# A new step table for one core that runs a gated linear-attention block and a gated MLP: another order and other engines for the same steps

## The chip, the core and the metric

The kernel runs on one core of one Trainium2 chip. Five engines work side by side, each through its own row of instructions, strictly in that row's order: TensorE (PE: matrix products and transposes, with its weight loads PEld), VectorE (DVE), ScalarE (ACT), GpSimd (POOL) and SyncE (SP, which here issues nearly all DMA transfers; ACT issues a few). An instruction waits until the steps that it depends on are done, and everything behind it in its engine's row waits with it. The metric is the device time of one execution in microseconds (us), as the median of several runs.

## What is computed

One transformer block with adaptive modulation, for 2048 rows of width 448 (bf16), cut to its core:

```python
mod = (silu(c) @ w_mod).reshape(1, 6, 1, 448)        # sa, ca, ga, sb, cb, gb
h = layernorm(x) * (1 + ca) + sa
q, k, v = split(h @ wqkv)                            # 16 heads of 28
phi = lambda t: concat(softmax(t @ w_phi), softmax(-(t @ w_phi)))
kv, z = einsum(phi(k), v), sum(phi(k))
o = phi(q) @ kv / (phi(q) @ z + 1e-6)
x = x + ga * (o @ wo)
h = layernorm(x) * (1 + cb) + sb
z1, z2 = split(gelu(h @ w_in))                       # 2 x 896
g = w_sp @ layernorm(z2) + b_sp                      # mixes the 2048 rows
x = x + gb * ((z1 * g) @ w_out)
```

## The kernel before

Everything stays on the chip between the stages. The 2048 rows are 16 tiles of 128 rows, and two tiles form a pair, so most loops run over 8 pairs. The function `fast_path` has one small function for each step, and the string `ORDER` (a step table) lists all steps of the program in one sequence. The loop at its end walks through `ORDER` and issues each step's instructions; every engine's row is thus the table read for that engine alone. A word is `step:arguments@bank/engine`: `kP:7,1/V` is step kP of pair 7, tile 1, on VectorE (V DVE, S ACT, G POOL, Y SP), `kM:0@A1` uses the two PSUM banks A1. A bank is free again only when the step that reads it out is done. DMA completion is told by a ring of eight semaphores: a transfer that is issued later in the table waits until the one eight places before it has landed.

The steps that matter below, in the order of the stages:

- **Start.** `ld:x0` to `x5` bring x (tiles 0, 1, 2-3, 4-7, 8-11, 12-15), `wq`, `wk`, `phi`, `v0` to `v3` the attention weights, `wca`, `wsa`, `wcb`, `wsb` four sixths of w_mod (wcb lands in the place of wca, wsb in that of wsa). `du` and `dh` are products of zeros that only keep TensorE busy. `ct` turns c, `ce` makes silu(c), `cf` (32 products) computes one sixth of the modulation, `ec` copies it out. `FTk`/`FTq` transpose wk and wq (line 817), `ETk`/`ETq` copy them out (821 on ACT, 823 on DVE), `bd` spreads phi over a block diagonal, `PFk`/`PFq` multiply (835), `EPk`/`EPq` copy the folded weights out (821, 823). In the trace f_ka holds wk first and f_qa holds wq first. `l1s`, `l1e`, `l1r`, `l1a` are the first layernorm (845, 849, 853, 857), `X` a transpose on TensorE for pairs 0 and 1 with `XE` (802 on ACT, 804 on DVE) as its modulating copy, `T1` a transpose by DMA for the other pairs with `md` (802, 804) behind it.
- **Keys.** For each pair `kM` and `vM` (910) are the products for keys and values, `kE` (917) the exponentials, `vC` (821, 823) the copy of the values, `kS` (927), `kR` (931) and `kP` (934) the normalisation, and `kA` (943) adds the pair to kv. `qM` (963) and `qE` (969) make the query side in eight parts. Behind `kA:7`, `kc` (949) and four `km` (953) turn kv into the right factor. `gr`, `ge` make the gate ga or gb, `wos` and `wts` (981) multiply it into wo and w_out.
- **Queries.** For each tile `nM` (994) is the numerator; for four tiles `nD` (1008) is the denominator, worked on by `nX` (821, 823), `nC` (1024), `nS` (1028), `nR` (1031), `nV` (1035); `nT` (1038) multiplies both, `nA` (1044) adds the halves, `T2` transposes by DMA, `wX`, `wM` (1055, 1063) multiply with wo, `wR`, `wQ`, `lA`, `lD`, `l2r`, `l2a` are the second layernorm, `X2`/`XF` and `T3`/`md:1` its transposes.
- **MLP.** `zM`, `zG`, `zQ`, `zA`, `zD`, `zW`, `zN` (1115 and on) make z2 and its layernorm, `yM`, `yG` (1132, 1136) z1, `W` (1141) transposes w_sp by DMA, and `tT`, `sS`, `pM` (1212), `pc`, `pb`, `u`, `cA`, `cX` are a seven-product scheme of the mixing product, `gM`, `gG` its plain part; `oM`, `oH` (1162, 1167) multiply with w_out, `oE`, `oG`, `oD`, `oF` add x and store.

Of the kernel before, what the change touches and what calls it, by code (L numbers as in the profile page):

```python
# [1367 lines left out]
```

## Time and profile before

| what | value |
|---|---|
| median of 3 runs (range) | 242.66 us (242.04 to 243.3) |
| the profiled execution, its own time | 243.4 us |
| its span, first to last instruction | 241.6 us |
| busy in the span | PE 230.8, DVE 191.4, POOL 129.0, ACT 112.8 us |
| instructions of the program | 6052 |
| first kM starts | 18.73 us |
| first zM starts | 82.65 us |
| last product's end to the span's end | 236.60 to 241.60 us |

PE is busy for nearly the whole span, so what counts is where it waits, and what it does that is no product of the result. The 1.8 us between the span and the own time lie outside the program's instructions. The page's groups give a mean duration for each line, engine and shape; a timeline row gives the start, the duration, the engine, the line and, in brackets, the idle time just before and what ended it.

### The profile page before, as it was taken

How to read it: one execution, taken by the hardware profiler on the slowest of the kernel's cores; microseconds unless marked ns; L12 is line 12 of the kernel's file. 1: busy time of each engine (PE TensorE's matmuls, PEld its weight loads, DVE VectorE, ACT ScalarE, POOL GpSimd, SP SyncE). 2: the span in 40 equal slices, each digit the busy share in tenths (PEclk: the TensorE clock that was granted, in tenths of full speed). 3: DMA queues.
4: the chain of work that ended last, by engine and by line, in shares of the span. 5: the costliest groups of instructions: out<-in, count | busy, mean ns of one | idle time of the engine just before them, and what ended most of it. 6: DMA issues, size and time to landing. Idle time of an engine off the chain costs nothing.

```text
span 241.6 us, 6052 instructions
## 1 busy us (share of the span) xinstructions
PE 230.8 (96%) x2501; PEld 127.1 (53%) x2501; DVE 191.4 (79%) x339; ACT 112.8 (47%) x201; POOL 129.0 (53%) x147
## 2 busy tenths in 40 slices
PE   7799999979999999999999999999999999999991
PEld 3687766558765555455444444444454445444551
DVE  3899999999999986847899983986899495439461
ACT  2779999786788999979876020000010000000000
POOL 1579779880578946454693079401699900035200
PEclk9999999999999999999999999999999999999997
DMA  7978988930056477889999500089900000000052
GB/s 186 280 194 201 172 181 266 292 77 3 3 81 117 80 145 184 160 135 178 175 173 184 76 0 0 1 151 158 171 0 3 0 0 0 11 29 19 29 174 59
DMA packets 64165, 26.27 MB, mean 109 GB/s; under 512 B 52865, under 2 KB 63106, under 8 KB 64130
## 3 DMA queue, kind: packets, MB, share of 16 engines
q1 hardware_dynamic: 62656, 24.72, 50.7%
q10 hardware_dynamic: 1474, 1.09, 1.4%
q8 instruction: 21, 0.34, 0.6%
q14 instruction: 14, 0.11, 0.2%
HBM read 11.22 MB, written 1.84 MB: 54 GB/s over the span
## 4 chain that ended last, share of the span: by engine, by line
PE 81%; DMA 8%; DVE 7%; POOL 1%; issue 1%; ACT 1%; DVEq 0%; ACTq 0%
PE f_psum L1212 30%; PE f_psum L1132 9%; PE f_psum L1162 8%; PE f_psum L1115 8%; PE f_psum L910 7%; PE f_psum L1149 6%; PE f_psum L1063 3%; PE f_psum L963 3%; DMA f_oo<-f_oo 3%; DMA f_wm<-in_w_mod_dram 3%; PE f_psum L786 2%; DMA f_ka<-in_A_wqkv_dram 2%; DVE f_ksum L927 2%; DVE f_qa L934 1%; DVE f_t L1038 1%; PE f_psum L994 1%
## 5 line engine op out<-in xcount | busy, mean ns | idle before, releaser
L1212 PEld LDWEIGHTS <-f_z2n 128*128 128x128 bf16 x192 | 18.6, 98 | 22.3 <-issue 0.4
L1212 PE MATMUL f_psum<-f_wsp,f_z2n 128*128 128x512 bf16 x120 | 27.2, 379 | 0.0
L1266 POOL TENSOR_TENSOR f_z1T<-f_z2g,f_z1T 128x512 bf16<-128x512 f32 x3 | 4.4, 1462 | 35.9 <-DVE f_z2g L1241 35.9
L1115 PE MATMUL f_psum<-f_win,f_hx 64*128 64x448 bf16 x224 | 22.3, 349 | 0.0
L1212 PE MATMUL f_psum<-f_hx,f_Eq 128*128 128x512 bf16 x96 | 22.0, 379 | 0.0
L1132 PE MATMUL f_psum<-f_hx,f_win 64*128 64x512 bf16 x196 | 21.6, 376 | 0.0
L1162 PE MATMUL f_psum<-f_wout,f_z1T 128*128 128x448 bf16 x105 | 20.8, 352 | 0.0
L969 ACT ACTIVATE f_Eq<-f_psum 128x1024 bf16<-128x1024 f32 x16 | 15.9, 1039 | 4.4 <-PE f_psum L963 4.3
L1038 DVE TENSOR_TENSOR f_t<-f_psum,f_bsp 128x896 bf16<-128x896 f32 x16 | 17.0, 1083 | 0.5 <-POOL f_oo L1044 0.2
L1115 PEld LDWEIGHTS <-f_hx 64*128 64x128 bf16 x224 | 11.5, 94 | 9.9 <-issue 0.2
L910 PEld LDWEIGHTS <-f_hx 64*128 64x128 bf16 x224 | 11.6, 94 | 9.1 <-issue 0.7
L927 DVE TENSOR_REDUCE f_ksum<-f_E 128x64 f32<-128x1792 bf16 x8 | 16.0, 1997 | 0.1
L1132 PEld LDWEIGHTS <-f_win 64*128 64x128 bf16 x196 | 9.7, 94 | 11.3
L1212 PEld LDWEIGHTS <-f_Eq 128*128 128x128 bf16 x96 | 9.4, 98 | 11.3
L1162 PEld LDWEIGHTS <-f_z1T 128*128 128x128 bf16 x105 | 10.3, 98 | 9.6
L1136 ACT ACTIVATE f_z1T<-f_psum 128x1024 bf16<-128x1024 f32 x14 | 14.0, 1023 | 2.8 <-PE f_psum L1132 2.7
L1120 ACT ACTIVATE f_z2n<-f_psum 128x896 bf16<-128x896 f32 x16 | 14.5, 911 | 1.7 <-PE f_psum L1115 1.7
L1234 ACT ACTIVATE f_hx<-f_psum 128x512 f32<-128x512 f32 x1 | 0.6, 597 | 30.5 <-PE f_psum L1212 30.5
L1178 DVE TENSOR_TENSOR f_x<-f_psum,f_x 128x448 bf16<-128x448 f32 x15 | 9.1, 621 | 7.0 <-PE f_psum L1162 7.0
L917 ACT ACTIVATE f_E<-f_psum 128x896 bf16<-128x896 f32 x16 | 13.9, 939 | 1.1 <-PE f_psum L910 0.5
L1044 POOL TENSOR_TENSOR f_oo<-f_t 128x448 bf16<-128x448 bf16 x9 | 9.4, 1049 | 9.0 <-DVE f_t L1038 9.0
L963 PE MATMUL f_psum<-f_hx,f_Wq 64*128 64x256 bf16 x224 | 13.9, 269 | 0.0
(190 smaller groups left out, 525.5 us busy)
## 6 DMA issues: line engine op xcount, KB each, us to landing
f_win<-in_B_w_in_dram SPq DMA_DIRECT2D x2, 1344.0 KB, 12.6
f_wm<-in_w_mod_dram SPq DMA_DIRECT2D x4, 392.0 KB, 8.1
f_x<-in_A_x_dram SPq DMA_DIRECT2D x3, 448.0 KB, 7.4
out_dram<-f_x SPq DMA_DIRECT2D x10, 112.0 KB, 1.8
f_ka<-in_w_mod_dram SPq DMA_DIRECT2D x2, 392.0 KB, 3.9
f_wout<-in_B_w_out_dram SPq DMA_DIRECT2D x1, 784.0 KB
f_wv<-in_A_wqkv_dram SPq DMA_DIRECT2D x2, 336.0 KB, 5.6
f_win<-in_A_wo_dram SPq DMA_DIRECT2D x2, 336.0 KB, 8.6
```

The lines of the kernel that those rows point to most:

```text
L910: nc.tensor.matmul(t[:, h, 0:D], lhsT=hT[HALF[h], p, j, :], rhs=w[HALF[h], at[h][j], :], start=(j == 0), stop=(j == NB - 1))
L927: nc.vector.tensor_reduce(out=ksum[:, 2 * p + t0:2 * p + t1], in_=Er[:, p % NR, t0:t1].rearrange("p t a s (f h) -> p (t a s) h f", h=2), a ...
L963: nc.tensor.matmul(t[:, h, u * 256:(u + 1) * 256], lhsT=Wq[HALF[h], j, 2 * c2 + u].rearrange("p h e -> p (h e)"), rhs=hT[HALF[h], 2 * st:2 ...
L969: nc.scalar.activation(out=Eq[st // 2][:, 2 * c2:2 * c2 + 2, s, o:o + 512].rearrange("p u (h q) -> p h u q", h=2), in_=ps["q" + str(n)].re ...
L1038: nc.vector.tensor_tensor(out=tr[i % 2].rearrange("p s (k h d) -> p k s h d", k=2, h=8), in0=numv(i)[:, :, :, :, 0:DH], in1=Sx[:, i, :, :, ...
L1115: nc.tensor.matmul(ps["z" + str(2 * p + h)][:, hf, 0:D], lhsT=hT[HALF[h], p, j, :], rhs=win[1][HALF[h], AT[h][j], hf * D:(hf + 1) * D], st ...
L1120: nc.scalar.activation(out=g, in_=ps["z" + str(i)][:, :, 0:D], func=ACT.Gelu_apprx_tanh, accum_out=zs1[:, i:i + 1])
L1132: nc.tensor.matmul(t[:, h, :], lhsT=win[0][HALF[h], AT[h][j], fc * P:(fc + 1) * P], rhs=hT[HALF[h], 4 * g:4 * g + 4, j, :], start=(j == 0) ...
L1136: nc.scalar.activation(out=z.rearrange("p (t h q) -> p h t q", h=2, q=P), in_=ps["y%d_%d" % (g, fc)].rearrange("p h (t q) -> p h t q", q=P ...
L1149: nc.tensor.matmul(g[:, 0, 0:b - a], lhsT=later["z2n"][:, s_, fc * P:(fc + 1) * P], rhs=wspT[t][:, s_, a:b], start=(s_ == 0), stop=(s_ == ...
L1162: nc.tensor.matmul(ps["o" + str(t)][:, 0, 0:D], lhsT=later["z1T"][:, fc, t * P:(t + 1) * P], rhs=wout_s[:, fc, :], start=(fc == 0), stop=( ...
L1212: nc.tensor.matmul(t[:, 0, :], lhsT=b[:, j, f * P:(f + 1) * P], rhs=a[:, j, :], start=(PSTART[k] and j == 0), stop=(j == NH - 1), skip_gro ...
```

## The change

Only the string `ORDER` is different. The same steps on the same data stand in another sequence, a part of them on another engine, some with another PSUM bank; the zero products `dh` are 12 and not 9. The first lines of the table:

```diff
-ld:x1/Y ld:wk/S du:4@1 ld:phi/Y ld:c/S ld:x0/Y ld:x2/Y ld:wq/Y du:4@1 ld:x3/Y ld:wca/Y ld:x4/Y du:1@1 l1s:1 ct@0 FTk:0@1 ce:1 ld:wsa/Y l1s:0 FTk:1@2 ETk:0/S
+ld:x2/Y ld:c/S du:4@1 ld:wq/Y ld:wk/S ld:x1/Y ld:x0/Y ld:phi/Y du:4@1 ld:wca/Y ld:x3/Y ld:wsa/Y du:1@1 ct@0 l1s:3 FTq:0@1 ld:x4/Y ce:1 l1s:2 FTq:1@2 dh:1@3
```

**Place 1, the start.** SP's row from its first transfer on: x1, phi, x0, x2, wq, x3, wca, x4, wsa and wcb before.

```order
L676 DMA f_x<-in_A_x_dram 128x448
L670 DMA f_phi<-in_A_w_phi_dram 112x4x28
L676 DMA f_x<-in_A_x_dram 128x448
L676 DMA f_x<-in_A_x_dram 128x2x448
L655 DMA f_qa<-in_A_wqkv_dram 112x4x448
L676 DMA f_x<-in_A_x_dram 128x4x448
L673 DMA f_wm_116<-in_w_mod_dram 112x4x448
```

The same place after the change: x2, wq, x1 and x0, phi, wca, x3, wsa.

```order
L676 DMA f_x<-in_A_x_dram 128x2x448
L655 DMA f_qa<-in_A_wqkv_dram 112x4x448
L676 DMA f_x<-in_A_x_dram 128x448 x2
L670 DMA f_phi<-in_A_w_phi_dram 112x4x28
L673 DMA f_wm_116<-in_w_mod_dram 112x4x448
L676 DMA f_x<-in_A_x_dram 128x4x448
L673 DMA f_wm_116<-in_w_mod_dram 112x4x448
```

The load of wq moved from the fifth place to the second, phi from the second to the fifth, wca ahead of x3. ACT's row at the same place before, with its two loads, the copies of the transposed weights (f_ka, f_qa), those of the folded ones (f_Wk, f_Wq) and the modulating copies XE (L802):

```order
L655 DMA f_ka<-in_A_wqkv_dram 112x4x448
L679 DMA f_c_row<-in_c_dram 1x448
L766 ACT_TABLE_LOAD
L766 ACTIVATE f_e<-f_psum 112x4
L821 COPY f_ka<-f_psum 112x896 x2
L821 COPY f_qa<-f_psum 112x896
L821 CAST f_Wk<-f_psum 128x448
L821 CAST f_Wk<-f_psum 128x896 x2
L821 CAST f_Wq<-f_psum 128x2x4x56 x5
L821 CAST f_Wk<-f_psum 128x896
L802 ACTIVATE f_hx<-f_psum,f_mod_81 128x128 x4
L821 CAST f_Wq<-f_psum 128x2x4x56
```

And after the change:

```order
L679 DMA f_c_row<-in_c_dram 1x448
L655 DMA f_ka<-in_A_wqkv_dram 112x4x448
L766 ACT_TABLE_LOAD
L766 ACTIVATE f_e<-f_psum 112x4
L821 COPY f_qa<-f_psum 112x896
L821 COPY f_ka<-f_psum 112x896
L821 COPY f_qa<-f_psum 112x896
L821 CAST f_Wk<-f_psum 128x896
L821 CAST f_Wq<-f_psum 128x2x4x56 x3
L821 CAST f_Wk<-f_psum 128x896 x2
L821 CAST f_Wq<-f_psum 128x2x4x56
L802 ACTIVATE f_hx<-f_psum,f_mod_81 128x128 x7
```

The copies begin with wq and not with wk, both copies of wq and one of wk are here, and all seven XE of pair 0 stand on ACT; the last cast of Wk comes behind them. On TensorE the order is FTq, one dh, FTk, five dh, PFk:2, `cf:1`, PFq:6 and PFq:0, PFk:0 and PFk:4, one dh, PFq:2, `cf:0`, the four X, four dh, PFk:6, PFq:4, `cf:3`, kM:0; before it was FTk, three dh, FTq, PFk:6, 4, 2, PFq:0, PFk:0, `cf:1`, PFq:2, six dh, PFq:6, `cf:0`, the X, PFq:4, `cf:3`, kM:0.

**Place 2, between the last kP and the first nT.** DVE's row before, from the last kP on (f_qa<-f_E); f_win holds wo here, f_KVbd is the result of km, f_t of nT.

```order
L934 TENSOR_TENSOR f_qa<-f_E,f_kr_119 128x16x56
L934 TENSOR_TENSOR f_qa<-f_E,f_kr_120 128x16x56 x2
L981 TENSOR_TENSOR f_win<-f_win,f_g_rep_121 128x896
L949 TENSOR_SCALAR f_psum<-f_psum 128x16
L953 TENSOR_TENSOR f_KVbd<-f_psum,f_mask 56x8x29 x4
L981 TENSOR_TENSOR f_win<-f_win,f_g_rep_121 128x448
L981 TENSOR_TENSOR f_win<-f_win,f_g_rep_121 128x896
L823 COPY f_bsp<-f_psum 128x256
L1024 TENSOR_TENSOR f_cr_99<-f_bsp 128x128
L1028 TENSOR_TENSOR f_dn_101<-f_cr_99 128x64
L1031 RECIPROCAL f_dn_101<-f_dn_101 128x64
L1035 TENSOR_TENSOR f_bsp<-f_bsp,f_dn_101 128x128
```

After the change the same stretch is shorter:

```order
L934 TENSOR_TENSOR f_qa<-f_E,f_kr_119 128x16x56
L934 TENSOR_TENSOR f_qa<-f_E,f_kr_120 128x16x56 x2
L949 TENSOR_SCALAR f_psum<-f_psum 128x16
L953 TENSOR_TENSOR f_KVbd<-f_psum,f_mask 56x8x29 x4
L823 COPY f_bsp<-f_psum 128x256
L1024 TENSOR_TENSOR f_cr_99<-f_bsp 128x128
L1031 RECIPROCAL f_dn_101<-f_dn_101 128x64
L1035 TENSOR_TENSOR f_bsp<-f_bsp,f_dn_101 128x128
```

The three wos (981) and the nS (1028) left DVE. POOL's row at that place before, from its last kP on:

```order
L934 TENSOR_TENSOR f_qa<-f_E,f_kr_119 128x16x56
L981 TENSOR_TENSOR f_win<-f_win,f_g_rep_121 128x896
L1044 TENSOR_TENSOR f_oo<-f_t 128x7x64
L1024 TENSOR_TENSOR f_cr_100<-f_bsp 128x128
L1028 TENSOR_TENSOR f_dn_102<-f_cr_100 128x64
L1044 TENSOR_TENSOR f_oo<-f_t 128x7x64
```

And after:

```order
L934 TENSOR_TENSOR f_qa<-f_E,f_kr_119 128x16x56
L981 TENSOR_TENSOR f_win<-f_win,f_g_rep_121 128x896 x2
L1028 TENSOR_TENSOR f_dn_101<-f_cr_99 128x64
L1024 TENSOR_TENSOR f_cr_100<-f_bsp 128x128
L1028 TENSOR_TENSOR f_dn_102<-f_cr_100 128x64
L981 TENSOR_TENSOR f_win<-f_win,f_g_rep_121 128x896
L1044 TENSOR_TENSOR f_oo<-f_t 128x7x64
L981 TENSOR_TENSOR f_win<-f_win,f_g_rep_121 128x448
```

All four wos are on POOL now, two of them ahead of nS:0. `ge:0`, for which the wos wait, comes from `gr:0`, which stands later on TensorE: behind kA:5 and directly ahead of kA:6 (before: behind kA:4, with two vM, kA:5 and a qM between it and kA:6).

Elsewhere, from kM:0 to the last kP, DVE has lost two vC, one XE of four instructions and one l1e, and gained one l1s, one kP and the reduction m5; POOL has gained four instructions of md, an l1a, two l1e and an l1r, and lost a kP and its memsets (m3, m4, m7 now stand ahead of kM:0). In the query stage a third qM (qM:6, qM:4 and qM:5) stands behind the first nD. On SP, two late loads moved back: `ld:u2`, a part of w_in, stands behind T2:2, and `ld:wmgb`, the data of `gr:1`, behind T2:3; one `W` of the mixing matrix moved forward into the key stage.

92 lines of the change are left out of this document (46 added, 46 removed).

## The prediction, made before the changed kernel had run

> **What bounds the kernel now.** The page's first part comes first, then the stages of the program in the view by windows.
>
> ```profile
> PE 230.8 (96%) x2501; PEld 127.1 (53%) x2501; DVE 191.4 (79%) x339; ACT 112.8 (47%) x201; POOL 129.0 (53%) x147
> ```
>
> ```profile
> 18.73:54.60 35.87, 34.36 (x491) 22.40 (x488) 35.13 (x52) 32.52 (x44) 29.82 (x34) 1.00 0.81 194
> 60.00:82.65 22.65, 21.54 (x578) 14.59 (x574) 21.86 (x37) 19.08 (x49) 17.41 (x25) 1.00 0.38 65
> 90.20:128.65 38.45, 38.45 (x379) 18.50 (x379) 29.07 (x65) 33.73 (x61) 24.37 (x29) 1.00 0.98 170
> 128.65:236.60 107.95, 107.95 (x538) 51.55 (x536) 79.50 (x104) 5.84 (x9) 43.55 (x31) 1.00 0.28 54
> ```
>
> The columns are the length, then the busy time of PE, PEld, DVE, ACT, POOL. From 90.20 us to the last product PE is busy all the time, so this order has nothing left to give there, and another one can only lose. In the keys (18.73 to 54.60) PE is idle 1.5 us while DVE is busy 35.13 of 35.87: DVE is the second bound. In the queries (60.00 to 82.65) both are nearly full. Who PE waits for stands in the view of waits:
>
> ```profile
> PE f_psum L943 <- DVE f_qa L934: 1.5, 1, 1.5
> ...
> PE f_psum L817 <- DMA f_qa<-in_A_wqkv_dram: 0.9, 1, 0.9
> PE f_psum L1063 <- DMA f_oo<-f_oo: 0.7, 2, 0.4
> PE f_psum L994 <- DVE f_t L1038: 0.7, 2, 0.5
> PE f_psum L786 <- DMA f_wm<-in_w_mod_dram: 0.4, 1, 0.4
> PE f_psum L1008 <- DVE f_KVbd L953: 0.2, 1, 0.2
> ```
>
> The products of the result are the same in both tables, and all that stand ahead of kM:0 before stand ahead of it after. So the end is the start of kM:0, plus the same products, plus zero products behind it, plus PE's waits behind it: 1.5 + 0.7 + 0.7 + 0.2 = 3.1 us now. These three, and the tail, are what the change can touch; the tail (last oE, oG, store) keeps its form.
>
> **The start.** PE's row and ACT's row up to kM:0:
>
> ```profile
> 5.65 1.53 PE L817 MATMUL f_psum<-f_ident,f_ka 112*112 112x112 bf16 x16
> 8.77 1.03 PE L817 MATMUL f_psum<-f_ident,f_qa 112*112 112x112 bf16 x16 [0.95 <-DMA f_qa<-in_A_wqkv_dram]
> 18.73 3.02 PE L910 MATMUL f_psum<-f_Wk,f_hx 64*128 64x448 bf16 x28
> ```
>
> ```profile
> 6.68 1.71 ACT L821 COPY f_ka<-f_psum 112x896 bf16<-112x896 bf16 x2 [0.76 <-PE f_psum L817]
> 10.23 2.15 ACT L821 CAST f_Wk<-f_psum 128x448 bf16<-128x448 f32 x3
> 13.52 2.44 ACT L821 CAST f_Wq<-f_psum 128x448 bf16<-128x448 f32 x5 [1.14 <-PE f_psum L835]
> 17.13 1.51 ACT L802 ACTIVATE f_hx<-f_psum,f_mod 128x128 bf16<-128x128 bf16 x4 [0.35 <-PE f_psum L874]
> 18.93 1.19 ACT L802 ACTIVATE f_hx<-f_psum,f_mod 128x128 bf16<-128x128 bf16 x3
> ```
>
> ACT begins with wk's copies at 6.68 now. After the change it begins with wq's. When wq lands follows from the transfers (size, median us from issue to landing):
>
> ```profile
> f_ka<-in_A_wqkv_dram ACTq DMA_DIRECT2D x1, 392.0 KB, 4.1
> f_qa<-in_A_wqkv_dram SPq DMA_DIRECT2D x1, 392.0 KB, 6.1
> f_x<-in_A_x_dram SPq DMA_DIRECT2D x1, 224.0 KB, 4.9
> f_phi<-in_A_w_phi_dram SPq DMA_DIRECT2D x1, 24.5 KB, 3.9
> ```
>
> wq landed just before its transposes at 8.77, as the last of some 1257 KB (wk 392, two tiles of x 224, phi 24.5, x2 224, wq 392); x2, 392 KB earlier in that count, landed about 1.7 us before it (its 4.9 us against wq's 6.1, issued half a microsecond apart). Ahead of it now stand x2 and, beside it, wk: 1008 KB with its own. That is 249 KB less, 249/392 of 1.7 us, so an estimate of 7.7. Sixteen transposes take 1.03 us, ETq:1 can start at 8.7. From there ACT has, ahead of kM:0: three copies of 0.86 (1.71 for two), three wide casts of 0.86 (2.15 for two and a half), five narrow ones of 0.49 (2.44 for five; four of Wq, the last of Wk), and seven XE (1.51 + 1.19): 2.6 + 2.6 + 2.4 + 2.7 = 10.3 us, with no wait 19.0, and with some handovers between PE and ACT **19.3 against 18.73: +0.6 us**. The zero products (five, one and four) stand where PE would wait for ACT in this chain, so they cost nothing here; if ACT were sooner, each would cost about 0.2. ETk:0 and one EPq are on DVE, beside it; phi, now behind 1257 KB, lands at about 8.7, and bd and ETk:0 on DVE are then done by 10.5, before ETq:0 on ACT. wca, 448 KB earlier in its queue, no longer holds `cf:1` (0.4 us of wait now), but ACT is later than that. Bounds: wq no sooner than wk now (4.8, all the rest of the chain then held by wsa and wcb as before) gives about -0.6; wq as late as now (8.7) gives +1.6.
>
> **The dummy behind kM:0.** One dh follows kM:0 (dh:1 behind km). Six took
>
> ```profile
> 13.61 1.47 PE L743 MATMUL f_psum<-f_zero 128*128 128x512 bf16 x6
> ```
>
> so one costs **+0.2**, or nothing if PE waits for km there.
>
> **The last kP.** Here PE's largest wait ends:
>
> ```profile
> 52.27 2.31 DVE L934 TENSOR_TENSOR f_qa<-f_E,f_kr 128x896 bf16<-128x896 bf16 x1
> 54.50 0.61 DVE L981 TENSOR_TENSOR f_win<-f_win,f_g_rep 128x896 bf16<-128x896 bf16 x1
> ```
>
> ```profile
> 52.07 2.02 POOL L981 TENSOR_TENSOR f_win<-f_win,f_g_rep 128x896 bf16<-128x896 bf16 x1 [0.90 <-ACT f_g_rep L978]
> ```
>
> ```profile
> L934 DVE TENSOR_TENSOR f_qa<-f_E,f_kr 128x896 bf16<-128x896 bf16 x9 | 7.2, 830 | 0.1
> L823 DVE CAST f_vaug<-f_psum 128x896 bf16<-128x896 f32 x2 | 2.1, 1062 | 0.0
> L804 DVE TENSOR_SCALAR f_hx<-f_psum,f_mod 128x128 bf16<-128x128 bf16 x5 | 1.4, 331 | 0.0
> L845 DVE BATCH_NORM_STATS2 f_st<-f_x 128x6 f32<-128x448 bf16 x4 | 2.5, 613 | 0.0
> ```
>
> kP:7,1 took 2.31 us where the other eight mean (9 x 830 - 2310)/8 = 645 ns, and it ended 0.5 us after POOL's wos did: it stood still for 1.7 us while POOL worked. Then a wos of 0.61 stood ahead of kc and km. After the change DVE up to the last kP has two vC less (2.1), four XE (1.3), and more by an l1s (about 0.8), a kP (0.6) and m5: about 1.8 us less. Behind it there is no wos; and POOL's first wos waits for gr:0 and ge:0, which now come with kA:6, that is, after kP:7,1 has begun. So DVE reaches km 1.8 + 1.7 + 0.6 = 4.1 us sooner, less the 0.6 of the start, and PE, which waits 1.5 + 0.2 us there, does not wait any more: **-1.7**. Next late are PE's own products, with qM:7 between kA:7 and nD:0 for the 1.9 us of kc and km. Bounds: nothing, if kP:7,1 meets a wos again, and -1.7, since no more wait stands there.
>
> [...]
>
> **The queries.** From nT:0 on DVE has the same work, and PE, which has one more qM (28 products) between nD:0 and the last nM, waits less for nT (0.7 now). wM's waits for the transposes (0.7) stay, since nA:15 goes to the slower POOL. I take **-0.5** between 0 and -1.4. `gr:1` needs wmgb, whose load of 392 KB is now issued only behind T2:3, near 71; such a load took 3.9 to 4.1 us, and gr:1 comes at about 76, so this is hidden with about a microsecond to spare. u2, which zM:0 needs, has some ten. The early `W` costs SP a place in a stretch where SP only waits.
>
> **The rest.** From 90.20 on no engine but PE is near full (at most 33.7 of 38.45 us in the third window's row, 79.5 of 107.95 in the fourth), and the change moves products of PE there but adds no instruction to it: I take 0, with nothing to gain, and a loss only by a hole that is not there now.
>
> Sum: 243.4 + 0.6 + 0.2 - 1.7 - 0.5 = 242.0 us for an execution like the profiled one. Its own time is 0.74 above the median of 242.66, so the median should be **241.3 us**, 0.6% less.
>
> **Rivals.** *The clock comes late* (0.20). At the start the products are slow: nine zero products
>
> ```profile
> 1.23 4.02 PE L738 MATMUL f_psum<-f_zero 128*128 128x512 bf16 x9 [1.23 <-DVE f_zero L706]
> ```
>
> take 0.45 each, six later ones 0.25, and the transposes at 5.65 change their pace within the row (1.53 against 1.03 us for the same sixteen). The clock column shows 1.00 all along, so it is these rows that show it. Now PE works from 1.23 to 7.8 with little idle; after the change nothing stands between ct (about 5.7) and wq (7.7), 2 us of idle. If PE stays slow up to `cf:1`, FT, dh and PFk:2 (about 4 us) take 1.8 times as long, 3.3 more, of which the five dh and ACT's copies hide half: +1.6, so 242.9. [...]
>
> *The relief does not come* (0.15): kP:7,1 meets a wos again because PE and ACT are sooner with gr:0 and ge:0 than DVE with kR:7. Then the 1.7 stay: 243.0. For it: ge:0 took half a microsecond and ACT has slack. Against it: gr:0 stands behind kA:5.
>
> *POOL becomes the bound, slower than before* (0.20). POOL has, from kM:0 up to nS:0:
>
> ```profile
> L934 POOL TENSOR_TENSOR f_qa<-f_E,f_kr 128x896 bf16<-128x896 bf16 x7 | 12.1, 1748 | 2.8 <-DVE f_kr L931 2.6 <-PE f_psum L943 0.2
> L804 POOL TENSOR_SCALAR f_hx<-f_hx,f_mod 128x256 bf16<-128x256 bf16 x8 | 5.1, 653 | 0.3 <-DMA f_hx<-f_hx 0.3
> L853 POOL TENSOR_TENSOR f_rs<-f_rs,f_mhalf 128x4 f32<-128x4 f32 x2 | 2.2, 1094 | 1.4 <-DVE f_nm L850 1.4
> L981 POOL TENSOR_TENSOR f_win<-f_win,f_g_rep 128x896 bf16<-128x896 bf16 x1 | 2.0, 2015 | 0.9 <-ACT f_g_rep L978 0.9
> ```
>
> The window's 29.8 us, one wos more (2.0), four md (2.6), an l1a and an l1r (1.8), a kP less (1.7): 34.5. nC:0 should be done near 56, so POOL may idle 2.2 us from 19.3 on; it idles 6.05 now. If it idles as much, nS:0 comes at 59.9, and through nR and nV
>
> ```profile
> 59.99 2.09 DVE L1038 TENSOR_TENSOR f_t<-f_psum,f_bsp 128x896 bf16<-128x896 f32 x2
> ```
>
> nT:0 at 61.3, 1.3 later than now; the queries follow DVE, nA:15 on POOL adds 0.6: 245.3, median 244.6. From 4.7 us of idle on it is slower than now. Against it: much of the idle is filled by the added steps themselves.
>
> **How the numbers follow.** Forecast 0.45, by its bounds 240.1 to 242.4. Two in ten may be left out: the range goes from 239.9 (all 3.1 us of waits gone with the start a little later) to 244.2, inside the last rival. About 0.5% (1.2 us) is what a measurement of this kernel can tell from no change. Faster by more has 0.42: most of the forecast, and the little of the clock's rival that ends low; within it 0.36: the forecast's upper end, the clock and the lost relief; slower 0.22: POOL, and the upper end of the clock.
>
> **What would show it.** kM:0 at 19.0 to 19.7 in PE's row and wq's transposes near 7.7; zero products behind 5.7 at 0.25 (clock) or 0.45; kP:7,1 at 0.6 and not 2.3; no wait of line 943; nT:0 near 58 and zM:0 near 81.5 (82.65 now); no wait of PE behind 90. Wrong it would be by a wait of several microseconds at `gr:1`, at nS:0 on POOL, or in the mixing product, where any hole is new.

## The result, and the profile after

The changed kernel takes 250.37 us (median of 6 runs, 249.01 to 252.34) beside 242.55 us for the kernel before (6 runs): a ratio of 1.0318, 95% interval 1.0275 to 1.0361. It is slower by 7.8 us, where 241.3 had been forecast with a range up to 244.2. Below, a ratio is always that to the kernel before on the same chip, and disturbed executions are left out of it, so it need not be the quotient of the two medians.

The page's first part after:

```profile
PE 232.6 (94%) x2490; PEld 126.9 (51%) x2504; DVE 186.4 (75%) x329; ACT 111.9 (45%) x197; POOL 132.7 (53%) x161
```

TensorE is busy 1.8 us more for the same products and three small dummies, in a span that is 6.9 us longer (248.5 beside 241.6); its own time is 250.43. Where the span grew is read from the view by windows, cut at the first product of kM:0, of nD:0 and of zM:0 and at the last product. After:

```profile
0.00:20.26 20.26, 16.59 (x276) 11.98 (x280) 12.69 (x42) 11.64 (x22) 10.58 (x28) 0.92 0.86 229
20.26:62.57 42.31, 37.31 (x499) 22.85 (x498) 38.01 (x52) 31.23 (x42) 33.27 (x39) 0.92 0.69 151
62.57:90.42 27.85, 26.09 (x745) 18.65 (x747) 24.54 (x46) 22.73 (x53) 20.74 (x31) 1.00 0.39 68
90.42:243.53 153.11, 152.58 (x986) 73.38 (x988) 110.80 (x191) 46.26 (x83) 68.07 (x65) 1.00 0.49 86
```

And the kernel before, cut at the same steps:

```profile
0.00:18.73 18.73, 16.18 (x277) 11.37 (x278) 13.21 (x47) 10.91 (x19) 9.64 (x24) 1.00 0.86 224
18.73:56.57 37.84, 36.30 (x529) 23.98 (x526) 37.01 (x57) 32.52 (x44) 29.82 (x34) 1.00 0.77 184
56.57:82.65 26.08, 24.79 (x719) 17.77 (x719) 24.96 (x45) 22.37 (x52) 17.41 (x25) 1.00 0.33 57
82.65:236.60 153.95, 153.50 (x996) 74.00 (x988) 115.83 (x193) 47.05 (x88) 72.16 (x66) 1.00 0.48 87
```

The first number behind the colon pair is the length. The start is 1.53 us longer, the keys 4.47, the queries 1.77, the MLP 0.84 shorter. One qM (28 products, 1.53 us at full clock) moved from the keys into the queries; with it put back, the keys lost 6.0 us and the queries 0.2. So the loss is in the keys, with the granted clock (the third number from the end) at 0.92 in the first two stages.

The view of TensorE's waits says on whom:

```profile
PE f_psum L943 <- DVE f_qa L934: 2.9, 3, 1.4
PE f_psum L817 <- DMA f_qa<-in_A_wqkv_dram: 1.8, 1, 1.8
...
PE f_psum L943 <- POOL f_qa L934: 1.2, 1, 1.2
```

kA (line 943) waits for kP (934) four times, 4.1 us in all, where it waited once for 1.5. DVE's row in that stretch, from the timeline:

```profile
43.55 3.94 DVE L934 TENSOR_TENSOR f_qa<-f_E,f_kr 128x896 bf16<-128x896 bf16 x1
...
54.59 0.55 DVE L931 RECIPROCAL f_kr<-f_ksum 128x64 bf16<-128x64 f32 x1
55.06 3.40 DVE L934 TENSOR_TENSOR f_qa<-f_E,f_kr 128x896 bf16<-128x896 bf16 x3
```

and POOL's:

```profile
42.61 1.10 POOL L804 TENSOR_SCALAR f_hx<-f_hx,f_mod 128x256 bf16<-128x256 bf16 x2
43.67 3.34 POOL L934 TENSOR_TENSOR f_qa<-f_E,f_kr 128x896 bf16<-128x896 bf16 x2
50.24 4.98 POOL L934 TENSOR_TENSOR f_qa<-f_E,f_kr 128x896 bf16<-128x896 bf16 x3 [3.23 <-DVE f_kr L931]
55.67 4.52 POOL L981 TENSOR_TENSOR f_win<-f_win,f_g_rep 128x896 bf16<-128x896 bf16 x2 [0.45 <-ACT f_g_rep L978]
```

The row at 43.55 is kP:4,0. The six kP on DVE ahead of it take 0.6 us each, this one 3.94. POOL is at work without a pause from before 43.55 to 47.01 (the last md, kP:3,1, kP:4,1), and kP:4,0 ends 0.48 us behind that. In the kernel before the same step ran as POOL's kP:4,1 was ending:

```profile
44.96 0.60 DVE L934 TENSOR_TENSOR f_qa<-f_E,f_kr 128x896 bf16<-128x896 bf16 x1
```

```profile
43.33 1.69 POOL L934 TENSOR_TENSOR f_qa<-f_E,f_kr 128x896 bf16<-128x896 bf16 x1 [0.97 <-DVE f_kr L931]
```

Back in the changed kernel, kS:5 to kR:7 stand behind kP:4,0 on DVE, so POOL in its turn waits 3.23 us for kR:5. At 55.06 the same again, smaller: of the three kP the last, kP:7,1, takes 2.29 us, across POOL's first wos.

TensorE's row shows what that does there:

```profile
53.63 0.63 PE L943 MATMUL f_psum<-f_vaug,f_qa 128*128 128x58 bf16 x16 [1.18 <-POOL f_qa L934]
54.10 0.92 PE L975 MATMUL f_psum<-f_ka,f_scb 112*128 112x448 bf16 x4
55.76 1.34 PE L943 MATMUL f_psum<-f_vaug,f_qa 128*128 128x58 bf16 x24 [0.74 <-DVE f_qa L934]
58.51 0.57 PE L943 MATMUL f_psum<-f_vaug,f_qa 128*128 128x58 bf16 x8 [1.41 <-DVE f_qa L934]
59.02 3.17 PE L963 MATMUL f_psum<-f_hx,f_Wq 64*128 64x256 bf16 x28
```

kA:5, kA:6 and kA:7 wait 3.33 us between them, and qM:7, the 28 products at 59.02, takes 3.17 us. The same 28 take 1.70 elsewhere in this trace. The view by windows, cut where the records of the granted clock change, shows the reason:

```profile
4.40:7.81 3.41, 1.59 (x22) 1.08 (x20) 1.08 (x5) 0.17 (x1) 2.35 (x7) 1.00 1.15 285
7.81:11.23 3.42, 3.42 (x25) 2.38 (x24) 2.25 (x5) 2.62 (x3) 0.65 (x1) 0.50 1.12 283
...
45.36:48.78 3.42, 2.65 (x56) 1.86 (x53) 3.42 (x2) 2.90 (x4) 1.65 (x2) 1.00 1.72 199
48.78:52.19 3.41, 3.41 (x48) 2.04 (x42) 3.20 (x4) 2.89 (x4) 1.95 (x2) 1.00 0.36 88
52.19:55.60 3.41, 1.66 (x24) 0.77 (x20) 3.31 (x4) 1.81 (x3) 3.03 (x2) 1.00 0.00 0
55.60:59.02 3.42, 1.85 (x33) 1.62 (x34) 2.86 (x3) 0.00 (x0) 3.35 (x2) 0.50 0.02 5
59.02:62.43 3.41, 3.16 (x30) 2.01 (x29) 1.78 (x5) 0.20 (x1) 1.17 (x1) 0.50 0.00 0
```

In this trace the granted clock changes at 7.81, 11.23, 55.60 and 62.43 us, each a whole multiple of 3.41 us behind its first record at 4.40. Of the stretches of that length between 4.40 us and the last product, those behind 1.59, 1.66 and 1.85 us of work ran at 0.50, and the others, all behind 2.65 us or more, at 1.00. So the clock is at half once behind the wait for wq at the start, and twice in a row behind the waits for kP.

That gave two theories for the 6 us in the keys. **A:** DVE's kP:4,0 stands still while POOL works through its row, and everything behind follows from it. **B:** the time is lost by the late start and by TensorE's clock, and a long kP:4,0 only fills a wait that is there anyway. For the clock itself: **C**, idle time halves it, against **D**, it doesn't hang on that.

### The profile page after: what moved, and what is told of

The parts are those of the page before. It is cut to its first block, busy times and chain, and to the rows that moved or that the text cites. A ratio compares the mean times of both kernels' runs of the same rounds, so it can differ in the third digit from the quotient of the medians.

```text
span 248.5 us, 6052 instructions
## 1 busy us (share of the span) xinstructions
PE 232.6 (94%) x2490; PEld 126.9 (51%) x2504; DVE 186.4 (75%) x329; ACT 111.9 (45%) x197; POOL 132.7 (53%) x161
## 4 chain that ended last, share of the span: by engine, by line
PE 72%; DVE 11%; DMA 7%; POOL 4%; issue 2%; ACT 1%; SPq 0%; DVEq 0%
PE f_psum L1212 29%; PE f_psum L1115 9%; PE f_psum L1132 9%; PE f_psum L1162 8%; PE f_psum L1149 6%; DMA f_hx<-f_hx 3%; DVE f_qa L934 3%; PE f_psum L963 3%; DVE f_ksum L927 3%; PE f_psum L1063 3%; DMA f_qa<-in_A_wqkv_dram 2%; DMA f_oo<-f_oo 2%; DVE f_st L845 2%; POOL f_hx L857 1%; PE f_psum L786 1%
## 5 line engine op out<-in xcount | busy, mean ns | idle before, releaser
L1266 POOL TENSOR_TENSOR f_z1T<-f_win,f_z1T 128x512 bf16<-128x512 f32 x13 | 15.8, 1227 | 27.0 <-DVE f_win L1241 27.0
L1162 PE MATMUL f_psum<-f_wout,f_z1T 128*128 128x448 bf16 x105 | 21.3, 352 | 0.0
L1234 ACT ACTIVATE f_Eq<-f_psum 128x512 f32<-128x512 f32 x4 | 2.4, 598 | 37.0 <-PE f_psum L1212 37.0
L1241 DVE SCALAR_TENSOR_TENSOR f_win<-f_psum,f_win 128x512 f32<-128x512 f32 x16 | 10.8, 684 | 10.0 <-PE f_psum L1212 10.0
L1115 PEld LDWEIGHTS <-f_hx 64*128 64x128 bf16 x224 | 10.9, 94 | 10.2
L910 PEld LDWEIGHTS <-f_hx 64*128 64x128 bf16 x224 | 10.5, 94 | 10.2 <-DVE f_hx L804 0.7
L963 PE MATMUL f_psum<-f_hx,f_Wq 64*128 64x256 bf16 x224 | 15.0, 287 | 0.0
L1237 POOL TENSOR_TENSOR f_win<-f_Eq,f_bsp 128x512 f32<-128x512 f32 x4 | 5.5, 1374 | 16.5 <-ACT f_Eq L1234 16.5
```

Of the source, the lines that this page charges most:

```text
L963: nc.tensor.matmul(t[:, h, u * 256:(u + 1) * 256], lhsT=Wq[HALF[h], j, 2 * c2 + u].rearrange("p h e -> p (h e)"), rhs=hT[HALF[h], 2 * st:2 ...
L1115: nc.tensor.matmul(ps["z" + str(2 * p + h)][:, hf, 0:D], lhsT=hT[HALF[h], p, j, :], rhs=win[1][HALF[h], AT[h][j], hf * D:(hf + 1) * D], st ...
L1162: nc.tensor.matmul(ps["o" + str(t)][:, 0, 0:D], lhsT=later["z1T"][:, fc, t * P:(t + 1) * P], rhs=wout_s[:, fc, :], start=(fc == 0), stop=( ...
L1266: eng.tensor_tensor(out=z, in0=src, in1=z, op=ALU.mult)
```

## The experiments

In each diff a fragment of the table stands before and after; nothing else in the kernel is changed. Lengths of stages are from the traced execution, cut as above.

**1. One step moved: kP:4,0 behind kR:5.**

```diff
-kP:4,0/V kP:4,1/G vC:5/S
+kP:4,1/G vC:5/S
...
-kR:5,0,2 ld:u3/Y
+kR:5,0,2 kP:4,0/V ld:u3/Y
```

> The changed table with one step moved: kP:4,0 on DVE stands behind kR:5 instead of ahead of kS:5. Theory A (DVE's kP:4,0 stood still for 3.3 us because POOL worked through kP:3,1 and kP:4,1 without a pause): kP:4,0 starts near 46.1 and ends near 47.5, so 1.4 us long instead of 3.94; kS:6 starts near 47.5 instead of 49.99, kR:7 ends near 52.7 instead of 55.14. If the wos on POOL don't stop the last kP for longer than now, nT:0 is near 63.7 instead of 66.16 and the time is 247.5 to 248; if they do, the gain is eaten there and the time is 249 to 250. Theory B (the time was lost at the start and by the half clock of TensorE, and DVE's long kP:4,0 only filled a wait): kR:7 ends near 55 all the same and the time stays at 250.4.

Measured: 244.35 us (10 runs), ratio 1.0057, interval 1.0014 to 1.0101. A single word of the table, in another place, is worth 6 us (250.37 to 244.35). DVE's row:

```profile
46.35 1.17 DVE L934 TENSOR_TENSOR f_qa<-f_E,f_kr 128x896 bf16<-128x896 bf16 x1
...
52.55 1.63 DVE L934 TENSOR_TENSOR f_qa<-f_E,f_kr 128x896 bf16<-128x896 bf16 x3
```

and POOL's and TensorE's:

```profile
43.70 8.66 POOL L934 TENSOR_TENSOR f_qa<-f_E,f_kr 128x896 bf16<-128x896 bf16 x5
54.46 3.72 POOL L981 TENSOR_TENSOR f_win<-f_win,f_g_rep 128x896 bf16<-128x896 bf16 x2 [2.10 <-ACT f_g_rep L978]
```

```profile
54.66 1.70 PE L963 MATMUL f_psum<-f_hx,f_Wq 64*128 64x256 bf16 x28
```

kP:4,0 meets only the end of kP:4,1 and takes 1.17 us; POOL has no pause for kR:5 any more. The three last kP take 1.63 us together, since gr:0 now comes late enough for the wos to start behind them, and qM:7 runs at full clock. The gain was twice what theory A had forecast, because the two later losses went with the first. From kM:0 to nD:0 it takes 36.43 us beside 42.31: 5.88 less. By steps: kR:7 ends 32.40 us behind kM:0 and not 34.88 (2.48); from there to the end of kP:7,1 it takes 1.54 and not 3.32 (1.78); from there to nD:0 2.49 and not 4.11 (1.62, the clock and a shorter wait). The start was as late as in the changed kernel (kM:0 at 20.24), so this run holds the start still. Theory B falls.

**2. The second stall alone: gr:0 and ge:0 behind kA:7.**

```diff
-kP:6,0/V gr:0@7 kP:7,0/V kA:6@6 kP:7,1/V ge:0 kA:7@6 wos:4,6/G
+kP:6,0/V kP:7,0/V kA:6@6 kP:7,1/V kA:7@6 gr:0@7 ge:0 wos:4,6/G
```

> The changed table with gr:0 and ge:0 moved behind kA:7, so that no wos runs on POOL during the last three kP. Theory A (kP:7,1 is stopped by POOL's wos:4,6): kP:7,1 takes 0.6 instead of 2.30 us, kA:7 ends near 57.4 instead of 59.08, km ends near 59.3 instead of 60.98; gr:0 costs TensorE 0.9 us between kA:7 and qM:7 that it had idle before, so nD:0 starts 0.8 to 1.7 us sooner and the time is 248.7 to 249.6. Theory B (kP:7,1 is long for another reason): it still takes 2.3 us, and the time is 250.4 to 251.3.

Measured: 249.11 us (4 runs), ratio 1.0291 (1.022 to 1.0362).

```profile
56.29 1.72 DVE L934 TENSOR_TENSOR f_qa<-f_E,f_kr 128x896 bf16<-128x896 bf16 x3
```

The three kP take 1.72 and not 3.40 us, so it was the wos that stopped kP:7,1. nD:0 comes 41.04 us behind kM:0, 1.3 less: the forecast of theory A. The intervals of the two ratios (this one and the changed kernel's 1.0275 to 1.0361) overlap, so this rests on the trace and not on the times. kP:4,0 took 3.94 us here too.

**3. Both.** The diff is that of 1 and 2 together.

> Both edits: kP:4,0 behind kR:5, and gr:0 with ge:0 behind kA:7. Theory A: the two gains add up, kR:7 ends near 52.7, kP:7,1 near 54.5 (58.46 in the changed kernel), and as TensorE's waits ahead of kA:5 to kA:7 shrink from 3.3 us in all, its clock stays full from 55.6 to 62.4, which is worth up to 1.5 us more: 244.7 to 246.5. Theory B: no more than 1 us less than the changed kernel, 249.4 or more.

Measured: 244.95 us (4 runs), ratio 1.0136 (1.0071 to 1.0201), within the forecast of theory A, but its "the two gains add up" was wrong. It is no better than the first edit alone, which had taken away the second stall already; what is left of the second edit is that gr:0 (0.92 us of TensorE) stands between kA:7 and qM:7. From kM:0 to nD:0 it takes 36.97 us beside 36.43.

**4. TensorE kept busy at the start: four dh between ct and FTq:0.**

```diff
-ct@0 l1s:3 FTq:0@1
+ct@0 dh:4@5 l1s:3 FTq:0@1
```

> The changed table with four zero products more, between ct and FTq:0, where TensorE waits 1.8 us for wq. Theory C (the granted clock is halved from 7.81 to 11.23 because TensorE stood idle from 5.2 to 7.0): the clock is full there, the sixteen FTk take 1.05 instead of 1.70 us, the dh behind them 1.0 instead of 1.94, PFk:2 starts near 11.1 instead of 11.70 and kM:0 near 19.4 instead of 20.26; the time is 249.3 to 249.8. Rival D (the clock at the start doesn't hang on this idle time): the clock is half for 3.4 us all the same, kM:0 starts at 20.3 to 20.5, and the time is 250.4 to 250.7. How much of an earlier kM:0 reaches the end is open too, as kP:4,0 waits for POOL: none at all would give 250.4.

Measured: 249.57 us (4 runs), ratio 1.0331 (1.026 to 1.0401).

```profile
7.84 0.99 PE L817 MATMUL f_psum<-f_ident,f_ka 112*112 112x112 bf16 x16
8.89 1.02 PE L743 MATMUL f_psum<-f_zero 128*128 128x512 bf16 x4
...
18.50 1.69 PE L910 MATMUL f_psum<-f_Wk,f_hx 64*128 64x448 bf16 x16
```

FTk takes 0.99 us (1.70 in the changed kernel), the dh 1.02 (1.94), and kM:0 starts at 18.50, 1.76 sooner, as theory C had it. But the time falls by 0.8 us only, and by the ratio (1.0331 beside 1.0318) that is no gain that can be told. The next run shows why, and that this one does not decide between C and D.

**5. The changed kernel once more, unchanged.**

> The changed kernel, unchanged, for a second trace, as the executions differ by how many windows TensorE's clock is halved (249.0 to 252.3). If the stall of kP:4,0 is a property of the order and not of one execution, it takes 3.9 us again, kP:7,1 2.3 us again, and the span from kM:0 to nD:0 is 40 to 42.4 us (42.31 in the first trace) by whether the clock is halved behind the waits ahead of kA:5 to kA:7 or not; the median is 249 to 250.5.

Measured: 250.04 us (4 runs), ratio 1.033 (1.0251 to 1.0409). In this trace kM:0 starts at 18.34 without any dh: FTq starts at 6.60 instead of 7.00, and FTk goes at full pace. Run 1 had the slow FTk behind an idle time of 1.20 us, run 3 the quick one behind 1.44, so in these two the length of the wait doesn't decide it. The time of the clock's first record sorts all the traces of the changed table and its variants. The first record of a full clock stands at 5.14 to 6.14 us in the seven (this one and runs 3, 4, 7, 10, 11, 12) in which kM:0 starts by 18.9. It stands at 10.27 to 13.22 in runs 1, 2 and 8, where the products are slow for longer (from 7.81 to 11.23 us run 1 gets through 30, and this trace through 76) and kM:0 starts at 19.83 to 21.42, and at 4.40 and 4.01 in the first trace and in run 6, where the wait for wq falls into the stretch behind it and the granted clock is then 0.50 for 3.41 us (kM:0 at 20.26 and 20.00). Four of the seven had the dh ahead of FTq:0 and three had not, so no run shows that the dh help at the start. The slow start is the fate of some executions and not of all. The stall is in both:

```profile
L934 DVE TENSOR_TENSOR f_qa<-f_E,f_kr x10: 561/614/3944, 27.4 to 54.5; 128x896 bf16<-128x896 bf16 x10
```

The three numbers are the shortest, median and longest of the ten kP on DVE in ns. From kM:0 to nD:0 it takes 42.11 us (42.31 in the first trace).

**6. TensorE kept busy in the keys: four, three and six dh ahead of kA:5, kA:6 and kA:7.**

```diff
-kA:5@6
+dh:4@7 kA:5@6
...
-kA:6@6
+dh:3@4 kA:6@6
...
-kA:7@6
+dh:6@4 kA:7@6
```

> The changed table with thirteen zero products more: four ahead of kA:5, three ahead of kA:6 and six ahead of kA:7, where TensorE stands idle (1.18, 0.74 and 1.41 us). The steps of DVE and POOL are unchanged. Theory C (the half clock from 55.6 to 62.4 comes from this idle time and costs about 1.5 us): the clock stays full there, the 28 products of qM:7 take 1.7 instead of 3.17 us, nD:0 starts 1.4 to 1.6 us sooner against kM:0, and the time is about 1.5 us less than that of the changed kernel: 248.6 to 249.2. Rival D (the clock drops for another reason, or the chain through DVE sets the start of nD:0 anyway): nD:0 doesn't move against kM:0 by more than 0.3 us, and the time is 250.2 to 250.8. kP:4,0 should stay at 3.9 us in both.

Measured: 249.5 us (4 runs), ratio 1.0289 (1.0228 to 1.0349).

```profile
54.00:60.00 6.00, 5.30 (x73) 3.24 (x73) 5.35 (x9) 0.82 (x2) 4.86 (x3) 1.00 0.02 3
```

```profile
57.96 1.70 PE L963 MATMUL f_psum<-f_hx,f_Wq 64*128 64x256 bf16 x28
```

The clock stays full (1.00 in the row), qM:7 takes 1.70 us, and nD:0 comes 39.98 us behind kM:0 and not 42.31: theory C, in the keys. Of these 2.3 us, 0.6 are not the clock's: kR:7 ends 34.26 us behind kM:0 and not 34.88, and nothing that kR:7 waits for stands behind these dh. From there to nD:0 it takes 5.72 us, and 7.43 and 6.99 in the two traces of the changed kernel, so the clock's price is 1.3 to 1.7 us, as forecast (1.5). kP:4,0 still took 3.92. At most 0.9 us of it reached the end, and the interval of the ratio overlaps that of the changed kernel, so by the time no gain is shown: from zM:0 on this trace is longer than the changed kernel's (154.53 beside 153.11 and 153.56), and a zM (line 1115) waits 0.98 us for DVE's modulating copies, which the changed kernel does not have.

**7. Another cure for the first stall: kP:4,1 on DVE, so that POOL has one kP in a row and not two.**

```diff
-kP:4,0/V kP:4,1/G vC:5/S
+kP:4,0/V vC:5/S
...
-kR:5,0,2 ld:u3/Y
+kR:5,0,2 kP:4,1/V ld:u3/Y
```

> The changed table with kP:4,1 moved from POOL to DVE, behind kR:5; kP:4,0 keeps its place ahead of kS:5. POOL then has one kP in a row (kP:3,1) where it had two. Theory A, in the size that the stall should have: kP:4,0 stands still until POOL's row has a pause, so until the end of kP:3,1 and not of kP:4,1; it takes 2.2 to 2.4 us instead of 3.94 (or 0.6 to 0.8, if DVE gets its turn already at the end of the md ahead of kP:3,1). kS:6 begins about 1 us sooner against kM:0, since DVE has 0.6 us more to do, and the time is 248.5 to 249.5. Theory B (the long kP:4,0 has nothing to do with POOL's work): it stays at 3.9, and with the added kP the time is 250.4 to 251.

Measured: 245.94 us (10 runs), ratio 1.0105 (1.0057 to 1.0154). DVE's row and POOL's:

```profile
41.95 2.28 DVE L934 TENSOR_TENSOR f_qa<-f_E,f_kr 128x896 bf16<-128x896 bf16 x1
```

```profile
42.07 1.68 POOL L934 TENSOR_TENSOR f_qa<-f_E,f_kr 128x896 bf16<-128x896 bf16 x1
46.99 5.14 POOL L934 TENSOR_TENSOR f_qa<-f_E,f_kr 128x896 bf16<-128x896 bf16 x3 [3.24 <-DVE f_kr L931]
```

With one POOL step less the stall is shorter by just that step: 2.28 us where 2.2 to 2.4 were forecast. The time gained more than forecast, because here too kP:7,1 then missed the wos and the clock stayed full.

**8. The moment at which DVE asks: m6 and scb on POOL behind kP:4,1 instead of ahead of kP:3,1.** kP:4,0 stays where the changed kernel has it.

```diff
-m6 kP:2,0/V
+kP:2,0/V
...
-scb kP:2,1/V
+kP:2,1/V
...
-kP:4,1/G vC:5/S
+kP:4,1/G m6 scb vC:5/S
```

> The changed kernel with POOL's m6 and scb behind kP:4,1 instead of ahead of kP:3,1; kP:4,0 on DVE stays ahead of kS:5. POOL's kP:3,1 now begins 0.9 us sooner, so DVE asks with kP:4,0 in the middle of kP:3,1 and not during the md ahead of it. Theory G (DVE gets its turn when the POOL step that it met ends, as at the two wos behind kP:7,1, where it did get in between): kP:4,0 takes 1.2 to 1.5 us instead of 3.94, kP:4,1 on POOL begins late by 0.4 us, the gain against the changed kernel is 2.5 us or more and the time 244.5 to 247. Theory H (DVE stands still until POOL's row pauses): kP:4,0 ends 0.5 us behind kP:4,1, so it takes 2.9 to 3.2 us, and the gain is about 1 us: 248.5 to 249.5.

Measured: 246.05 us (4 runs), ratio 1.0123 (1.0049 to 1.0197). DVE's row and POOL's:

```profile
43.36 1.46 DVE L934 TENSOR_TENSOR f_qa<-f_E,f_kr 128x896 bf16<-128x896 bf16 x1
```

```profile
42.66 3.71 POOL L934 TENSOR_TENSOR f_qa<-f_E,f_kr 128x896 bf16<-128x896 bf16 x2
```

DVE asks at 43.36, in the middle of kP:3,1, and gets its turn when that ends; kP:4,1 stands back for it (POOL's pair takes 3.71 and not 3.34 us). Theory G. So the same DVE step against the same two POOL steps costs 0.9 us or 3.3 us by when it asks. In the changed kernel it asks 0.12 us ahead of the start of kP:3,1, with the last md still under way on POOL, and is passed over when kP:3,1 begins and again when kP:4,1 does. What decides there is not shown. kP:7,1 met the wos here too and took 2.30 us, so the second stall needs less than the whole of the first.

**9. The kernel before with its gate late: the term of -1.7 by itself.** ge:0 stands behind qE:7,0, so that POOL's wos cannot meet kP:7,1, and DVE's wos:4,6 behind nV:0.

```diff
-kP:6,0/V ge:0 kP:7,0/V kP:7,1/V kA:6@4 qE:7,0 wos:4,6/V kA:7@4
+kP:6,0/V kP:7,0/V kP:7,1/V kA:6@4 qE:7,0 ge:0 kA:7@4
...
-nV:0/V nT:0
+nV:0/V wos:4,6/V nT:0
```

> The kernel before with the gate of wo later: ge:0 stands behind qE:7,0 on ACT, so that POOL's wos:2,4 cannot run during kP:7,1, and DVE's wos:4,6 stands behind nV:0 instead of ahead of kc. This measures the prediction's term of -1.7 us by itself. If the term was right: kP:7,1 takes 0.6 instead of 2.31 us, km ends near 55.2 instead of 56.94, nT:0 starts near 59.1 instead of 59.99 (0.9 of the 1.7 us arrives, as a wos of 0.6 us now stands ahead of nT:0), and the time is 240.8 to 241.8 beside 242.5 for the kernel before. If TensorE's own row is the next limit: kP:7,1 is short, but nT:0 and the time stay within 0.3 us of before.

Measured: 242.09 us (10 runs) beside 242.84, ratio 1.0014 (0.9969 to 1.0058): no difference that can be measured, and the hoped-for 0.9 us (0.9963) lies just outside the interval.

```profile
52.39 1.62 DVE L934 TENSOR_TENSOR f_qa<-f_E,f_kr 128x896 bf16<-128x896 bf16 x3
```

The stall is gone (three kP in 1.62 us), and nT:0 starts 7.60 us behind the end of kR:7 and not 8.65. The local gain of 1.05 us is there; in the traced execution the clock was halved from 18.59 to 22.00, and kR:7 ended 1.45 us later behind kM:0 than in the kernel before (34.07 beside 32.62), which hid it. Whether it reaches the end in other executions stays open.

**10. Both repairs: kP:4,0 behind kR:5 and four dh at the start.** The diffs of 1 and 4.

> Both repairs that helped alone: kP:4,0 behind kR:5, and four zero products in TensorE's wait for wq. If the two are independent, kM:0 starts at 18.5 to 19.0 and the span from kM:0 to the end is that of the first repair alone (222.9 us), so the time is 243.1 to 243.5, against 244.35 with the first repair alone; the ratio to the kernel before is 1.000 to 1.004. If a late kM:0 cost nothing any more, it would stay at 244.35. If the other edits of the table brought the 2.2 us that the prediction counts on behind kM:0, the time would be 240.5 to 241.5.

Measured: 243.67 us (10 runs), ratio 1.0055 (1.0025 to 1.0085), a little above the forecast. kM:0 starts at 18.73, and from there to the end of the span it takes 223.9 us and not 222.9. So of the 1.5 us that kM:0 came sooner than in run 1, 1.0 was lost again behind it, and the ratio (1.0055 beside 1.0057) is that of the first repair alone: that the two are independent is not shown. The third possibility, that the other edits bring the 2.2 us counted on behind kM:0, is ruled out. TensorE's waits behind kM:0:

```profile
PE f_psum L910 <- DVE f_hx L804: 0.8, 1, 0.8
PE f_psum L943 <- DVE f_qa L934: 0.8, 1, 0.8
PE f_psum L879 <- POOL f_hx L857: 0.7, 1, 0.7
PE f_psum L1115 <- DVE f_hx L804: 0.6, 1, 0.6
PE f_psum L879 <- DVE f_m L1083: 0.6, 1, 0.6
```

These five make 3.5 us; the kernel before had 3.1, at other places.

**11 and 12. The waits that are left: POOL's kP:4,1 sooner (m6 and scb behind it), and also T1:2,3 ahead of T1:3,4.** To the two repairs, the m6 and scb edit of 8 is added, then

```diff
-T1:2,3 l1a:11/G
+l1a:11/G
...
-l1a:5/G cf:3@7
+l1a:5/G T1:2,3 cf:3@7
```

> The two repairs (kP:4,0 behind kR:5; four zero products ahead of FTq:0) and, new, POOL's small steps m6 and scb behind kP:4,1 instead of ahead of kP:3,1. POOL then comes to the end of kP:4,1 0.9 us sooner against kM:0, just before DVE asks for its turn with kP:4,0. Theory A: kP:4,0 takes 0.6 to 0.8 us instead of 1.2 to 1.4, kA:4 waits 0.2 instead of 0.78 us, and as DVE is the limit there the gain of 0.5 us reaches nD:0: 243.0 to 243.3 beside 243.67 for the two repairs. Rival: TensorE's own products set nD:0 by now, and the 0.5 us stay in a wait behind: 243.5 to 243.8.

> The same, and T1:2,3 ahead of T1:3,4 on SP (in front of cf:3 in the table instead of behind qM:0), as the kernel before has it. kM:2 waits 0.7 to 0.8 us for md in the changed kernel and its variants, because the two transposes by DMA are issued together behind l1a:6. If that wait is lost time: md starts about 1 us sooner, kM:2 doesn't wait, and the time is 242.3 to 242.8, equal to the kernel before or a little under it. If DVE and not TensorE sets kA:5 to kA:7, the wait of kM:2 goes and comes back at kA:4: 243.0 to 243.4.

Measured: 243.72 us, ratio 1.0061 (1.0022 to 1.0099), and 243.82 us, ratio 1.0063 (1.0029 to 1.0096), 11 runs each. The waits of kA:4 and kM:2 went as intended: kM:0 to nD:0 takes 36.38 and then 35.63 us (36.75 without). Nothing of it reached the end: run 11 is within its rival's forecast, and run 12 is above both of its own. In run 12, zM:0 starts at 82.04, 0.6 us sooner than in the kernel before, and then the same wait as in run 6 comes up:

```profile
PE f_psum L1115 <- DVE f_hx L804: 1.2, 1, 1.2
```

From zM:0 to the last product it takes 154.82 us there, and 153.61 in run 11. So run 12's second forecast was right that the time comes back, but not about the place: it is behind zM:0, at DVE's copies for the second layernorm's tiles. Run 11's trace has no such wait; where its gain goes stays open.

**13. The kernel before once more, unchanged.**

> The kernel before, unchanged, for a second trace. Its profiled execution took 243.4 us, 0.7 to 0.9 above its medians, and single executions lie between 240 and 243.9, while those of the repaired tables lie within 0.5 us of 243.7. Theory E (the start varies: when wq, wca and wcb land): the second trace differs from the first by kM:0 (between 17.5 and 19.5), and the span behind kM:0 is 222.9 us within 0.3. Theory F (the span behind kM:0 varies, with waits in the queries or the mixing product): kM:0 is at 18.7 within 0.3 and the rest differs by 1 us or more.

Measured: ratio 1.0024 (0.9984 to 1.0063). Its second trace has the same stages as the first within 0.15 us each (kM:0 at 18.64, then 37.72, 26.13 and 154.00 us to the last product), so neither E nor F explains the executions at 240 to 241 us, of which no trace exists.

No version here beats the kernel before. What is left between it and the repaired tables, 0.6%, stays open: their traced executions take as long (242.95 us for the second trace of before, 243.21 for run 11), and the difference is in the untraced ones.

## Why the prediction was wrong, step by step

**The frame held.** The end was written as the start of kM:0 plus the same products plus dummies plus TensorE's waits. That is where the loss is: in the start, in the waits of kA, and, not foreseen at this place, in the products' own pace.

**The start** (19.3 forecast, bounds 18.1 to 20.3; 20.26 and 18.34 in two traces). The transposes of wq began at 7.00 and 6.60 and not at 7.7. From there to kM:0 11.6 us had been forecast; it took 13.26 in the first trace and 11.74 in the second, where the clock was full. So the rival "the clock comes late" was right in size in the first trace (1.6 us forecast, 1.5 measured) and absent in the second; that the clock comes late, and is not halved again after a first rise, is what runs 1, 2 and 8 had (first record of a full clock at 10.27 to 13.22 us). That the idle time ahead of wq makes it late is shown by no run: FTk was slow behind 1.20 us of it in run 1, and quick behind 1.44 in run 3.

**The last kP** (-1.7 forecast) is the step that failed, in two sentences of it. The first is that DVE reaches km "4.1 us sooner": the last km ended 2.5 us later, counted from kM:0 (40.72 beside 38.22). That figure was a sum of work on DVE alone. It took over durations (0.6 us for each kP) from rows of the old order, while the same part of the text had just shown that this step's duration depends on what POOL does at that moment. The rows of the new order that put kP:4,0 ahead of kS:5, where POOL has kP:3,1 and kP:4,1 behind each other, are not read in it. In the kernel before, kP:4,0 stood behind kS:5, and was done in 0.60 us just when POOL came free; here it took 3.94. Even without the stall the sum was too large: in run 1 the last km ends 36.38 us behind kM:0, 1.8 sooner than before and not 4.1, and kR:7 only 0.2 sooner (32.40 beside 32.62), so the 1.8 us of work taken off DVE hardly showed. The second is that gr:0 comes too late for a wos to meet kP:7,1. In a kernel without the first stall that is so (run 1), but with DVE 2.5 us late it came in time: the rival "the relief does not come" (0.15) happened, as a consequence. The halved clock behind these waits, 1.3 to 1.7 us (run 6), is not in the sum at all.

**The size of the collisions.** The highest of the rivals' sums, 244.6, is 3.3 us above the forecast. The runs put the collisions between DVE and POOL at 5.88 us in the keys: 2.48 by the first stall, 1.78 by the second that it brought about, 1.62 by TensorE's clock and the wait behind. The first had no place among the rivals' sums.

**What a relief is worth.** Even with both stalls gone the -1.7 did not arrive. In run 1 TensorE's wait of 1.5 us at kA:7 is gone as forecast, but the 0.2 at nD:0 is 0.31, and 0.71 at kM:2 and 0.78 at kA:4 are new; with the moved qM put back, the keys are 0.1 us longer than before.

**The queries** (-0.5 forecast, 0 to -1.4): 0.2 longer, with gr:1 in time as forecast in the first trace. **The dummy** behind km (+0.2) stands ahead of nD:0 and so is part of the keys; in the second trace it begins 0.32 us ahead of nD:0, near its forecast. **The rest** (0): 0.8 and 0.4 us shorter in the two traces. **POOL as the bound** (0.20): right about the sign of the result, wrong about the mechanism; nS:0 began 0.08 us behind nC:0, and POOL stood idle 4.28 us ahead of it.

## What to carry to other kernels

When a new order is judged by sums of durations from the old one, first mark the instructions whose duration depends on another engine (here DVE steps of 0.6 us that had once taken 2.3), and read in the new order, place by place, what that other engine does at the same time. A stall on the engine that is nearly full was not paid once here: it left TensorE idle, its granted clock was 0.50 for the 6.83 us from 55.60 on (1.00 there in run 6, with products of zeros in the gaps), and later steps were shifted into a new collision (kP:7,1 at 2.29 us). A wait removed in one stage counts only as far as the next stages' own chains are not the limit: here 1 us won ahead of nD:0 was given back in a wait of zM.

## What was not expected of the hardware

- The price of the collision between DVE and POOL hung on less than a microsecond of timing: kP:4,0 took 3.94 us where it asked 0.12 us ahead of POOL's kP:3,1, and 1.46 in run 8, where it asked 0.70 us into it. The kP of DVE that asked while a kP or a wos of POOL was under way ran when that step ended (0.65 us in all in run 11, with 0.17 of the step left, to 2.31 in the kernel before, with 1.81 left). One that asked 0.12 us before POOL started its kP, with an md still under way, stood through that kP (2.28 us in run 7), and where two followed each other through both (3.92 to 3.94 us in five traces). Why is not shown.
- TensorE's clock was halved in the keys without any long pause: in the first trace the longest wait there was 1.41 us, but stretches of 3.41 us with 1.66 and 1.85 us of work were followed by half clock, and one with 2.65 us of work was not. The kernel before came close to it, at its wait for the last kP (the two rows below): with 1.94 us of work, and 1.87 in its second trace, the next stretch still ran at full clock. So in these three traces the most work in a stretch at full clock with half clock behind it was 1.66 us, and the least with full clock behind it 1.87, as far as the records of products are complete. With thirteen products of zeros in the gaps the clock was 1.00 from 54 to 66 us (run 6).

```profile
51.15:54.56 3.41, 1.94 (x46) 1.52 (x40) 3.41 (x5) 2.67 (x4) 2.04 (x2) 1.00 0.02 7
54.56:57.98 3.42, 3.17 (x106) 2.74 (x108) 3.23 (x10) 1.27 (x2) 0.00 (x0) 1.00 0.00 0
```

- Once the clock was halved with no idle time in the records ahead of it. In run 9, TensorE is shown busy for 3.41 of the 3.41 us up to 18.59, and then comes the row below. In 2.05 us of that stretch cf's products of a single column run, which the view counts as busy like any other; whether that is the reason is not shown.

```profile
18.40:22.00 3.60, 3.60 (x25) 1.54 (x24) 3.46 (x12) 2.54 (x7) 3.60 (x7) 0.53 1.14 226
```
